# Attention and expert layer on one core: row maxima of pairs 2 to 8 handed on in two pieces, and three pieces of early work moved between engines

## The chip, the core and the metric

The kernel runs on one core of a Trainium2 chip. The core has five engines, each with its own instruction stream that runs in order: TensorE (PE, matrix products into PSUM), VectorE (DVE), ScalarE (ACT), GpSimd (POOL) and SyncE (SP, which here issues most of the DMAs). The metric is the device time of one execution in microseconds, lower is better.

## The reference, cut to what matters

```python
q_pool = q.reshape(B, H, S // 2, 2, D).mean(axis=3)       # B 8, H 8, S 1152, D 64
scores = scale * np.matmul(q_pool, k.transpose(0, 1, 3, 2))   # 576 queries x 1152 keys
scores = scores - np.max(scores, axis=-1, keepdims=True)
attn = np.exp(scores); attn = attn / (np.sum(attn, axis=-1, keepdims=True) + 1e-09)
x = np.matmul(attn, v)         # to (B * 576, 512), token major
# then a layer of 8 experts: each token goes to the expert with the largest
# logit (x @ w_gate + bias of its modality), 512 -> 1024 -> 512 with a ReLU,
# and is weighted with that expert's softmax probability
```

## The kernel before, in words

**Pairs and steps.** The 64 heads are worked in 32 pairs, numbered from 0; the two heads j=0 and j=1 of a pair lie in the upper and lower 64 partitions. `attention` writes a program in 18 steps per pair, 576 in all. Three steps make the scores of three key chunks of 128 for all 576 queries of one head: four PSUM banks of 432 columns, each a pair of products (L1051, L1052). So a pair has 36 products of L1051, the first 18 for j=0, and its first one marks the pair's start in the trace. ACT turns each bank into exponentials (L1053, `Pe`), and the lower halves of the exponentials' bits become a second f16 operand `Pl` (`lower`, L1034 on ACT or L1036 on DVE): of 1728 columns, 1152 go to ACT and 576 to DVE, but for pair 0 (`P_LIST = {0: 2}`) both pieces go to ACT. The value products (`pv`, L1110 to L1112, groups of three) follow some steps later.

**Maxima.** A product needs a bound of each query's scores first, which is the row maximum. `maxpass` makes it for one pair as 21 pieces: for each of nine groups u of 128 queries two products of 512 keys (L984), each reduced by one DVE instruction (L985), and for the last 128 keys three products with up to four groups side by side (L992, L993). These go through three PSUM buffers `pm`. `row` then reduces three numbers per query (L935), turns them with a small product (L949), scales them (L958, tile `mr`), and SP copies the result into row 64 of the operand `B2` (L959), which L1052 reads. For pair 1 (`TWO_ROWS = (1,)`) this is done twice: after five groups (1x5x128, enough for head j=0) and after nine (1x4x128, wanted by j=1); for other pairs once (1x9x128). Pair 0's first five groups are a prologue of their own (`first_max`, L1007, L1008), after `sum_q` has added the two query halves in two pieces.

**Order.** PE's order is written out by the string of a step in `ORD`: M is one piece of the maxima queue `mxq`, X a variable number of pieces, s a score bank, v a group of value products. M stands three times in three steps, X once in each. The pieces of a pair enter `mxq` from step 18p - 24 on. `at`, `later` and `later_end` place everything else at step numbers; SP's and POOL's instructions stand in the order in which they are written, and wait only for data.

```python
advance(mxq, 3 if t < T_F else 1 if t < X_ALL or t % (X_IN if t < X_SOME else 4) == 0 or len(mxq) > 1 else 0)
need(p, *(("place",) if p else ()), "row5" if j == 0 and (p == 0 or p in TWO_ROWS) else "row9")
```

The first line is the X of step t; the second, in `scores`, says which of the rows must have been written into the program. `place` and `place_rest` copy a pair's operands to where the products read them (L739, 12 DMAs a pair for pair 2), and `load_hi` loads f16 keys of pair 4 and later by a DMA from POOL's queue (L795). After the attention the experts run (`experts`), from about 720 us on.

Of the kernel before, what the change touches and what calls it, by code (L numbers as in the profile page):

```python
# [16 lines left out]
ALU = mybir.AluOpType  # L17
# [37 lines left out]

LOWS = (((0, 1152, 'A', 2), (1152, 1728, 'D', 3)), ((0, 1152, 'A', 2), (1152, 1728, 'D', 3)))
LOWS_LAST = (((0, 864, 'D', 1), (864, 1728, 'D', 3)),)
P_LIST = {0: 2}
LOWS_LIST = [tuple(((0, 1152, 'A', 2), (1152, 1728, e, 3)) for e in x) for x in ('DDA', 'DA', 'A')]
D0 = 5  # L60
T_RT = (20, 35, 43, 61)
D2 = (1, 0, 0, 0, 3)
T_K2 = 0
T_F = 7
T_P2 = 1
T_P1 = 8
T_M1 = 5
# [4 lines left out]
T_CAST = -36  # L72
# [73 lines left out]
DONE = object()  # L146
ORD = ('NvJMvsvMsvXF', 'JvvsMvvXFvv', 'vFvvsJvXv')
FIRST = (0, 1)
T_PRE = 2
TWO_ROWS = (1,)  # L150
X_ALL = 8
X_SOME = 105
X_IN = 3
T_MX2 = -23
T_MX3 = -23
FIN = 0
# [541 lines left out]
def attention(tc, ctx, att, ident, npairs, xpool, on_two, on_split, on_scale, jobs, side, set_pm, started, ahead, hip, own_port):  # L698
# [3 lines left out]
    nc = tc.nc  # L702
# [38 lines left out]
    half_q = lambda i: slice(i * 288, (i + 1) * 288)  # L741
# [409 lines left out]
    mxq, pvq, scq = [], [], []  # L1151
# [20 lines left out]
    def advance(q, n):  # L1172
        for _ in range(n):
            while q and next(q[0], DONE) is DONE:
                q.pop(0)
# [16 lines left out]
    def busy(n, w=512):  # L1192
        for _ in range(n):
            nc.tensor.matmul(idle[:, 0:w], zero[:, 0:P], zero[:, 0:w], start=True, stop=True, skip_group_check=True)
# [22 lines left out]
    first = first_max(0)  # L1217
    both = st[0]["q"].rearrange("p (w n) -> p w n", w=2)

    def sum_q(i):  # L1220
        nc.vector.tensor_tensor(both[:, 0, half_q(i)], both[:, 0, half_q(i)], both[:, 1, half_q(i)], op=ALU.add)
        nc.scalar.copy(qb[0:D, half_q(i)], q0[0:D, half_q(i)])

    sum_q(0)
    for i in range(3):
        split_hi(0, i)
        if i == 2:
            sum_q(1)
        for _ in range(2):
            next(first)  # L1230
        if i < 2:
            busy(1 + i)
    nc.scalar.copy(st[0]["qh"], q0)
    nc.scalar.copy(qb[D:P, SQ:S], q0[D:P])
    for i in (3, 4, 5, 6, 0, 1, 2):
        split_lo(0, i)
    st[0]["B1"] = pa.tile([P, 2 * KQ], F16, name="B1")
    place_k(0, (0,))
# [34 lines left out]
    mxq.append(maxpass(0, mp0))  # L1273
    for _ in range(T_PRE):
        advance(mxq, 1)
    busy(1)
    for t, f in zip(T_RT, started):
        at(t, 0, f)

    for p in range(npairs):  # L1280
        b = NSTEP * p
        go = lambda t, f, *a, p=p, b=b, **k: at(b + t, p, lambda: f(p, *a), **k)
        if p > 1:
            d = D2 if p == 2 else (0,) * 5
            if p < 4:
                go((T_K2, T_K3)[p - 2] - b, load_kq, end=False)
            go(T_SPLIT[p > 2] + d[0], split_q)
            go(T_QH[p > 2] + d[1], split_qh)
            if p > 3:
                go(T_CAST, load_hi)  # L1290
            else:
                for i in range(2):
                    go(T_HI[i] + d[2], split_hi, i)
            for i in range(3):
                go(T_LO[p > 2][i] + d[3], split_lo, i)
            go({2: T_MX2, 3: T_MX3}.get(p, T_MAX), lambda p: mxq.append(maxpass(p)), end=False)
            go(T_PLACE + (T_P2 if p == 2 else 0), place, end=False)
            if p > 2:
                go(T_REST, place_rest, end=False)
            go(T_LV[max(0, min(p, 4) - 2)], load_v)  # L1300
        elif p:
            go(T_P1 - b, place, end=False)
            go(T_M1 - b, lambda p: mxq.append(maxpass(p)), end=False)
            go(T_LV[max(0, min(p, 4) - 2)], load_v)
        sq, power_, vh, vs, vl = (T_SQ, T_POW, T_VH, T_VS, T_VL) if p > 1 else V1
        if p == 0:
            at(VS0, 0, lambda: shifted(0))
            continue
        if p == 1:
            go = lambda t, f, *a, p=p: at(t, p, lambda: f(p, *a))  # L1310
        go(sq, square)
        go(power_, power)
        for i, t in enumerate(vh):
            go(t, values, i, False)
        go(vs, shifted)
        for i, t in enumerate(vl):
            go(t, values, i, True)
# [14 lines left out]
    for t in range(NSTEP * npairs):  # L1332
        p, c18 = divmod(t, NSTEP)
        now[0] = t
        if jobs and c18 in JOBS:
            running.append(jobs.pop(0))
        for a in ORD[t % len(ORD)]:
            if a == "J":
                running[:] = [g for g in running if next(g, DONE) is not DONE]
            elif a == "F":  # L1340
                flush(t)
            elif a == "M":
                advance(mxq, 1)
            elif a == "X":
                advance(mxq, 3 if t < T_F else 1 if t < X_ALL or t % (X_IN if t < X_SOME else 4) == 0 or len(mxq) > 1 else 0)
            elif a == "N":
                scq.append(scores(p, *divmod(c18 // 3, 3)))
            elif a == "s":
                advance(scq, 1)
            elif a == "v":  # L1350
                advance(pvq, 2 if len(pvq) > 2 else 1)
        ends(t)
        if side and t >= wait:
            r = next(side[0], DONE)
            if r is DONE:
                side.pop(0)
            else:
                wait = t + (r or 1) if (r or 1) > 0 else NSTEP * npairs + r
# [484 lines left out]
```

## Time and profile before

| | us |
|---|---|
| median of three runs (1108.71 to 1110.17) | 1109.09 |
| the profiled execution's own time | 1109.55 |
| its span in the profile | 1107.8 |
| PE, DVE, ACT, POOL busy in the span | 1094.6, 951.4, 880.1, 449.2 |

The span is that of the instructions of one execution. PE's busy time counts matmuls whose ends are modelled and overlap, so a stretch in which PE is called busy can still hold small waits; how far apart two instructions start is the better measure. An idle time in square brackets in the rows below names what ended it.

### The profile page before, as it was taken

Reading aid. Unit: us, or ns where it says so; the run is one execution under the profiler, and the core shown is the slowest. Engines: PE = TensorE matmul, PEld = TensorE weight load, DVE = VectorE, ACT = ScalarE, POOL = GpSimd, SP = SyncE. Lnnn points to the kernel's source line nnn. Section 1 sums busy time; section 2 is a strip of 40 time slices with the busy share of each in tenths; the row PEclk is TensorE's granted clock in tenths of the full one; section 3 lists DMA queues with packets and bytes.
Section 4 is the critical chain, followed back from the end, with each engine's and each line's share of the span. In section 5 each row is a group of like instructions: output and inputs, shape, how many; then the busy total and the mean of one; then the engine's idle time right before and its main releaser. Section 6 shows DMA issues by size and latency. Waiting matters only on the chain. (4 is left out here: it accounts for less than half of the span.)

```text
span 1107.8 us, 36760 instructions
## 1 busy us (share of the span) xinstructions
PE 1094.6 (99%) x15134; PEld 812.5 (73%) x15134; DVE 951.4 (86%) x1897; ACT 880.1 (79%) x1397; POOL 449.2 (41%) x484
## 2 busy tenths in 40 slices
PE   8999999999999999999999999999999999999998
PEld 4777777777777777777777777876677667667666
DVE  8899999999999999999999999888987666756751
ACT  6999999999999999899999999876656565655652
POOL 8765444454545455545544454132122232121111
PEclk9999999999999999999999999999999999999999
DMA  8788867777678678687786775699989999999970
GB/s 252 184 189 213 200 174 192 198 196 195 171 212 203 174 197 205 162 205 179 214 190 174 213 160 120 185 298 313 275 257 232 304 312 289 272 279 270 280 209 33
DMA packets 178356, 237.59 MB, mean 214 GB/s; under 512 B 91555, under 2 KB 127027, under 8 KB 178180
## 3 DMA queue, kind: packets, MB, share of 16 engines
q1 hardware_dynamic: 168004, 207.12, 67.9%
q0 software_dynamic: 10176, 28.05, 11.4%
q8 instruction: 120, 1.97, 0.8%
q14 instruction: 56, 0.46, 0.2%
HBM read 158.43 MB, written 18.99 MB: 160 GB/s over the span
## 5 line engine op out<-in xcount | busy, mean ns | idle before, releaser
L1053 ACT ACTIVATE Pe<-psc 128x432 int32<-128x432 f32 x768 | 383.0, 526 | 51.0 <-PE psc L1052 32.2
L985 DVE TENSOR_REDUCE mp<-pm 128x1 f32<-128x512 f32 x566 | 372.9, 684 | 13.6 <-PE pm L984 6.8
L1111 PE MATMUL xp<-VS,Pl 128*128 128x65 f16 x2880 | 374.6, 194 | 0.0
L1110 PE MATMUL xp<-VH,Pe 128*128 128x65 f16 x2880 | 372.9, 193 | 0.0
L1112 PE MATMUL xp<-vl,Pe 128*128 128x64 f16 x2880 | 370.4, 191 | 0.0
L1111 PEld LDWEIGHTS <-Pl 128*128 128x128 f16 x2880 | 267.2, 97 | 86.3
L1051 PE MATMUL psc<-B 128*128 128x432 f16 (+2 forms) x1152 | 301.8, 285 | 0.9 <-ACT Pe L1053 0.8
L1052 PE MATMUL psc<-B 128*128 128x432 f16 (+5 forms) x1152 | 301.7, 286 | 0.0
L1110 PEld LDWEIGHTS <-Pe 128*128 128x128 f16 x2880 | 271.3, 98 | 41.0 <-issue 2.9
L1112 PEld LDWEIGHTS <-Pe 128*128 128x128 f16 x2880 | 268.8, 98 | 0.0
L1034 ACT ACTIVATE Pl<-Pe 128x1152 f16<-128x1152 uint16 x192 | 220.6, 1149 | 6.1
L984 PE MATMUL pm<-hi,QB 128*128 128x512 f16 x566 | 213.7, 378 | 1.9 <-DVE mp L985 1.2
L1497 PE MATMUL ph<-xpart,w1l 128*128 128x256 f16 x544 | 148.3, 273 | 0.0
L1496 PE MATMUL ph<-xpart,w1h 128*128 128x256 f16 x544 | 148.3, 273 | 0.0
L1495 PE MATMUL ph<-xpart,w1h 128*128 128x256 f16 x544 | 148.3, 273 | 0.0
L818 POOL TENSOR_TENSOR lo<-rawk,hi 128x576 f16<-128x576 f32 (+1 forms) x68 | 83.2, 1225 | 155.3 <-DVE Pl L1036 131.1
L1052 PEld LDWEIGHTS <-B 128*128 128x128 f16 (+1 forms) x1152 | 112.0, 97 | 23.0 <-issue 1.3
L1051 PEld LDWEIGHTS <-B 128*128 128x128 f16 x1152 | 111.5, 97 | 5.8 <-issue 0.7
L918 POOL TENSOR_SCALAR VH<-rawv,scales 128x512 f16<-128x512 f32 (+1 forms) x63 | 109.1, 1733 | 15.6 <-DVE Pl L1036 13.9
L1501 DVE SCALAR_TENSOR_TENSOR hl<-ph,hh 128x512 f16<-128x512 f32 x72 | 49.7, 690 | 70.3 <-ACT hh L1500 55.6
L1500 ACT ACTIVATE hh<-ph 128x512 f16<-128x512 f32 x72 | 43.0, 597 | 81.3 <-PE ph L1497 81.3
L1614 PE MATMUL po<-w2h,hl 128*128 128x512 f16 x280 | 106.1, 379 | 0.0
(326 smaller groups left out, 1885.5 us busy)
## 6 DMA issues: line engine op xcount, KB each, us to landing
w2r<-in_w_dram SPq DMA_DIRECT2D x72, 512.0 KB
w1r<-in_w_dram SPq DMA_DIRECT2D x68, 512.0 KB
rawv<-in_att_dram SPq DMA_DIRECT2D x32, 576.0 KB
B<-hi SPq DMA_DIRECT2D x128, 144.0 KB
rawq<-in_att_dram SPq DMA_DIRECT2D x31, 576.0 KB
rawk<-in_att_dram SPq DMA_DIRECT2D x31, 576.0 KB
B<-qh SPq DMA_DIRECT2D x128, 72.0 KB
B<-lo SPq DMA_DIRECT2D x64, 144.0 KB
```

Of the source, the lines that this page charges most:

```text
L984: nc.tensor.matmul(pm, QB[p % 2][:, u], s["hi"][:, t * 512:(t + 1) * 512], start=True, stop=True)
L985: nc.vector.tensor_reduce(mp[:, u, t:t + 1], pm, op=ALU.max, axis=AX.X)
L1034: nc.scalar.activation(low, rest, AF.Copy, scale=LOW)
L1051: nc.tensor.matmul(o, b1[:, ks], b1[:, qs], start=True, stop=False, skip_group_check=True)
L1052: nc.tensor.matmul(o, b2[:, ks], b2[:, qs], start=False, stop=True, skip_group_check=True)
L1053: nc.scalar.activation(Pe[:, D + x0:D + x1], pt, AF.Exp, scale=1.0 / 16)
L1110: nc.tensor.matmul(out, Ph[:, qs], vh[:, c, j, 0:D + 1], start=c == 0 and g == 0, stop=False, skip_group_check=True)
L1111: nc.tensor.matmul(out, Pl[:, qs], vs[:, c, j, 0:D + 1], start=False, stop=False, skip_group_check=True)
L1112: nc.tensor.matmul(out[:, 0:D], Ph[:, qs], vl[:, c, j], start=False, stop=c == NKC - 1, skip_group_check=True)
L1495: nc.tensor.matmul(o, hi[:, c, fs], xh[:, :, c], start=c == 0, stop=False)
L1496: nc.tensor.matmul(o, hi[:, c, fs], xl[:, :, c], start=False, stop=False)
L1497: nc.tensor.matmul(o, lo[:, c, fs], xh[:, :, c], start=False, stop=c == 3)
```

## The change

Six things change. (1) `TWO_ROWS` becomes pairs 1 to 7, so six more pairs (the second to the eighth, without the one that had it) hand on their maxima in two pieces, each with an L935, L949, L958 and L959 of its own. (2) The rate of X: three pieces a step only in steps 0 and 1 (was 0 to 6), one piece a step until step 7 as before, then one in steps divisible by 4 (was 3), and the extra piece when two pairs are in the queue only from step 105 on. One piece (was two) stands ahead of the first step. (3) Pair 0's lower halves of 576 columns go to DVE. (4) The second `sum_q` runs on POOL, behind two of POOL's four key splits in place of on DVE. (5) One filler product (`busy(1)`) ahead of the first step goes. (6) `load_hi` of pairs 4 to 9 stands five steps later.

```diff
-P_LIST = {0: 2}
+P_LIST = {}
-T_F = 7
+T_F = 2
-T_PRE = 2
-TWO_ROWS = (1,)
+T_PRE = 1
+TWO_ROWS = tuple(range(1, 8))
-X_IN = 3
+X_IN = 4
-    def sum_q(i):
-        nc.vector.tensor_tensor(both[:, 0, half_q(i)], both[:, 0, half_q(i)], both[:, 1, half_q(i)], op=ALU.add)
+    def sum_q(i, eng):
+        eng.tensor_tensor(both[:, 0, half_q(i)], both[:, 0, half_q(i)], both[:, 1, half_q(i)], op=ALU.add)
         nc.scalar.copy(qb[0:D, half_q(i)], q0[0:D, half_q(i)])
-    sum_q(0)
+    sum_q(0, nc.vector)
     for i in range(3):
         split_hi(0, i)
         if i == 2:
-            sum_q(1)
+            for k in (3, 4):
+                split_lo(0, k)
+            sum_q(1, nc.gpsimd)
...
-    for i in (3, 4, 5, 6, 0, 1, 2):
+    for i in (5, 6, 0, 1, 2):
         split_lo(0, i)
...
     for _ in range(T_PRE):
         advance(mxq, 1)
-    busy(1)
...
             if p > 3:
-                go(T_CAST, load_hi)
+                go(T_CAST + (5 if p - 2 in TWO_ROWS else 0), load_hi)
...
-                advance(mxq, 3 if t < T_F else 1 if t < X_ALL or t % (X_IN if t < X_SOME else 4) == 0 or len(mxq) > 1 else 0)
+                advance(mxq, 3 if t < T_F else 1 if t < X_ALL or t % (X_IN if t < X_SOME else 4) == 0 or len(mxq) > 1 and t >= X_SOME else 0)
```

On POOL, in the prologue (`rawq` are the queries, `rawk` the keys, `lo` their second f16 part), the difference is:

```order
 L1197 MEMSET B_1_113 1x1152
-L818 TENSOR_TENSOR lo<-rawk,hi 128x288 x4
+L818 TENSOR_TENSOR lo<-rawk,hi 128x288 x2
+L1221 TENSOR_TENSOR rawq<-rawq 128x288
+L818 TENSOR_TENSOR lo<-rawk,hi 128x288 x2
 L818 TENSOR_TENSOR lo<-rawq,qh 128x192 x3
 L771 TENSOR_TENSOR rawq<-rawq 128x576
```

The sum of the second query halves stands third in this group, and DVE's stream lost it.

On DVE, in pair 0 from the end of its second group of maxima on, there stood before:

```order
L993 TENSOR_REDUCE mp<-pm 128x4
L935 TENSOR_REDUCE m_393<-mp 128x4
L929 TENSOR_SCALAR VS_124<-VH_123 128x18x64
L958 TENSOR_SCALAR mr<-pj 4x128
L985 TENSOR_REDUCE mp<-pm 128x1 x8
L993 TENSOR_REDUCE mp<-pm 128x4
```

and there stands now:

```order
L935 TENSOR_REDUCE m_392<-mp 128x4
L1036 TENSOR_SCALAR Pl_116<-Pe_115 128x576
L929 TENSOR_SCALAR VS_124<-VH_123 128x18x64
L958 TENSOR_SCALAR mr<-pj 4x128
L985 TENSOR_REDUCE mp<-pm 128x1 x4
L1036 TENSOR_SCALAR Pl_118<-Pe_117 128x576
L985 TENSOR_REDUCE mp<-pm 128x1 x4
L993 TENSOR_REDUCE mp<-pm 128x4
L1036 TENSOR_SCALAR Pl_120<-Pe_119 128x576
```

Lower halves (L1036) now stand between the reductions; pair 0 has six of them.

On SP, around the rows of pair 1 (`mr` into B_1_113) and the copies for pair 2 (into B_0_111 and one more `B`), there stood before:

```order
L739 DMA QB_112<-qh 64x576 x2
L959 DMA B_1_113<-mr 1x5x128
L761 DMA rawv<-in_att_dram 128x1152
L959 DMA B_1_113<-mr 1x4x128
L756 DMA rawq<-in_att_dram 128x1152
L757 DMA rawk<-in_att_dram 128x1152
L739 DMA B_0_111<-qh 64x576 x2
L739 DMA B_924<-qh 64x576 x2
L739 DMA B_924<-lo 64x576 x2
L739 DMA B_0_111<-lo 64x1152 x2
L739 DMA B_924<-hi 64x1152 x4
L190 DMA wg<-in_w_gate_dram 128x4x8
```

and there stands now:

```order
L761 DMA rawv<-in_att_dram 128x1152
L959 DMA B_1_113<-mr 1x5x128
L739 DMA B_0_111<-qh 64x576 x2
L739 DMA B_893<-qh 64x576 x2
L739 DMA B_893<-lo 64x576 x2
L739 DMA B_0_111<-lo 64x1152 x2
L739 DMA B_893<-hi 64x1152 x4
L190 DMA wg<-in_w_gate_dram 128x4x8
L192 DMA bias<-in_bias_dram 128x16
L194 DMA idt<-in_ids_dram 128x72
L761 DMA rawv<-in_att_dram 128x1152
L959 DMA B_1_113<-mr 1x4x128
```

Pair 1's second row was ahead of pair 2's twelve copies and now stands behind them, three small loads and a load of values.

## Rows read from the trace of the kernel before

**Rows 1.** The page's busy us, share of the span and instructions by engine.
```profile
PE 1094.6 (99%) x15134; PEld 812.5 (73%) x15134; DVE 951.4 (86%) x1897; ACT 880.1 (79%) x1397; POOL 449.2 (41%) x484
```

**Rows 2.** Busy time by stretch: pair 0, pair 1, pairs 2 to 6, pairs 8 and 9.
```profile
16.69:41.87 25.18, 22.97 (x302) 15.64 (x301) 22.01 (x46) 22.49 (x39) 19.20 (x17) 1.00 0.77 222
41.87:66.48 24.61, 23.42 (x398) 17.82 (x397) 23.21 (x47) 22.21 (x37) 16.39 (x12) 1.00 0.73 175
66.48:175.64 109.16, 108.85 (x1896) 84.51 (x1895) 104.86 (x219) 100.69 (x170) 57.89 (x73) 1.00 0.81 196
197.53:240.84 43.31, 43.31 (x764) 33.76 (x763) 41.52 (x88) 40.06 (x68) 21.88 (x23) 1.00 0.75 189
```

**Rows 3.** Groups of PE instructions by line, from 16.69 to 66.48 us.
```profile
L1110 PE MATMUL xp<-VH,Pe 128*128 128x65 f16 x159 | 21.3, 193 | 0.0
L984 PE MATMUL pm<-hi,QB 128*128 128x512 f16 x47 | 17.4, 378 | 1.2 <-DVE mp L985 1.2
L992 PE MATMUL pm<-hi,QB 128*128 128x128 f16 x22 | 2.4, 218 | 0.6 <-DVE mp L985 0.6
```

**Rows 4.** Timeline of PE: start us, us, then the instruction.
```profile
9.79 0.34 PE L1007 MATMUL pm<-hi,QB 128*128 128x384 f16 x1 [1.14 <-DVE mp L1008]
...
23.05 0.34 PE L1051 MATMUL psc<-B 128*128 128x432 f16 x1 [0.48 <-ACT Pe L1053]
...
23.42 0.81 PE L984 MATMUL pm<-hi,QB 128*128 128x512 f16 x3
...
32.11 0.27 PE L949 MATMUL pm<-ident,m 128*5 128x128 f32 x1
32.22 0.19 PE L1110 MATMUL xp<-VH,Pe 128*128 128x65 f16 x1
...
32.30 0.19 PE L1110 MATMUL xp<-VH,Pe 128*128 128x65 f16 x1
...
41.87 0.35 PE L1051 MATMUL psc<-B 128*128 128x432 f16 x1
...
54.38 0.34 PE L1051 MATMUL psc<-B 128*128 128x432 f16 x1
```

**Rows 5.** Timeline of POOL.
```profile
6.86 2.10 POOL L818 TENSOR_TENSOR lo<-rawk,hi 128x288 f16<-128x288 f32 x3 [0.85 <-ACT hi L802]
...
48.56 1.11 POOL L912 TENSOR_TENSOR vl<-rawv,VH 128x512 f16<-128x512 f32 x1
```

**Rows 6.** Timeline of DVE.
```profile
8.28 0.99 DVE L1221 TENSOR_TENSOR rawq<-rawq 128x288 f32<-128x288 f32 x1
...
16.41 4.85 DVE L985 TENSOR_REDUCE mp<-pm 128x1 f32<-128x512 f32 x8
...
41.68 0.28 DVE L958 TENSOR_SCALAR mr<-pm 4x128 f16<-4x128 f32 x1
...
48.59 1.41 DVE L1036 TENSOR_SCALAR Pl<-Pe 128x576 f16<-128x576 uint16 x1
```

**Rows 7.** Timeline of ACT.
```profile
21.90 0.68 ACT L1034 ACTIVATE Pl<-Pe 128x576 f16<-128x576 uint16 x1
```

**Rows 8.** Instructions of L1036 up to 110 us: ns min/median/max, first and last start.
```profile
L1036 DVE TENSOR_SCALAR Pl<-Pe x17: 446/450/1407, 48.6 to 108.9; 128x576 f16<-128x576 uint16 x17
```

**Rows 9.** Timeline of SP's queue: each start is when the DMA is issued.
```profile
37.53 0.77 SPq L959 DMA_DIRECT2D B<-mr  x1
...
41.99 0.66 SPq L959 DMA_DIRECT2D B<-mr  x1
...
43.70 2.50 SPq L739 DMA_DIRECT2D B<-qh  x4
46.30 3.28 SPq L739 DMA_DIRECT2D B<-lo  x4
49.69 3.81 SPq L739 DMA_DIRECT2D B<-hi  x4
...
55.31 0.37 SPq L761 DMA_DIRECT2D rawv<-in_att_dram  x1
```

## The prediction, made before the changed kernel was run

> **What bounds the kernel now.** I read the page's busy times first: PE is busy in 99% of the span, DVE in 86% [rows 1]. So the end can come earlier in two ways only: less work on PE, or fewer waits of PE. The change takes one filler of 512 columns from PE and adds six small turns, so any gain has to come from waits, and the next view is the busy time by stretch, cut where pairs start [rows 2]. Pairs 8 and 9 take 43.31 us with PE busy in all of it: 21.66 us a pair is PE's own pace. Pairs 2 to 6 take 21.83 us each, close to it. Pairs 0 and 1 take 25.18 and 24.61 us. They don't hold the same work, so I counted it: 159 groups of value products, 46 maxima products of 512 keys and 22 of 128 (a product that straddles the border makes 47 of the 46) [rows 3], where two steady pairs have 180, 36 and 18. The price of each is the distance between starts: 0.08 us for a group, (0.81 - 0.38) / 2 = 0.215 for a product of 512 keys, a quarter of that for one of 128, 0.11 for a turn [rows 3, 4]. At PE's own pace the two pairs would take 43.31 - 21 x 0.08 + 10 x 0.215 + 4 x 0.054 + 2 x 0.11 = 44.2 us. They take 49.79, so **5.6 us are lost in waits before 66.48 us**, and 1.1 us more in the prologue, in the one wait there that this change touches (the product at 9.79) [rows 4]. After that almost nothing is left to win: 109.16 - 5 x 21.66 = 0.9 us in pairs 2 to 6, and from pair 7 on the two programs have the same work in the same order.
>
> **The prologue.** The product at 9.79 waits for the second half of the queries. DVE adds it from 8.28 to 9.27, behind four reductions. POOL has its second split done at 6.86 + 0.70 = 7.56, and a sum of the same 288 columns, taken at the split's 0.70, ends at 8.26 [rows 5, 6]. That is 1.0 us earlier, and DVE, whose reductions follow without a gap, gets 0.9 to 1.0 back. I take -0.9 for the start of pair 0; the bounds are 0 (if the sum meets DVE's reads) and the whole wait, -1.1. The filler lies just ahead of the first scores: -0.2 there at most; the first exponential waits for other work of the same chain, so I count none of it.
>
> **Pair 0.** Six lower halves go from ACT, where one lasts 0.68 us [rows 7], to DVE, where one lasts 0.45 when nothing is beside it. The waits for ACT, as the one at 23.05 [rows 4], should go. DVE gives up three reductions (25 products of 512 keys are issued ahead of pair 1 now, from 2 at pair 0's start; before it was 29, from 3), a group of short ones and a row, 3 x 0.60 + 0.68 + 0.45 [rows 6] (a row is 0.28 at L958 and, as an estimate from that, 0.17 at the smaller L935), and takes 6 x 0.45: 22.01 - 2.9 + 2.7 = 21.8 us. PE has 62 groups there and less of the maxima, 20 us. So neither engine keeps pair 0 at 25 us. One thing may: at 48.59 a lower half took 1.41 us, while POOL worked on one instruction from 48.56 to 49.67, and POOL is busy for 19.20 us of pair 0 [rows 2, 5, 6]. Of 17 lower halves up to 110 us the median is 0.45 and the longest 1.41 [rows 8], so I add 6 x 0.4 (between none and 0.96 each, nearer to the median): DVE 24.2 us if it waits for nothing else, of which 1.5 can lie behind PE's back, in the three buffers `pm`.
>
> The Trainium skill (SBUF — State Buffer, Who interferes with whom) says that such a DVE instruction and one of GpSimd exclude each other for the whole instruction, whoever comes first. The long row agrees; by the rule alone, with POOL busy three quarters of the time, all six would wait and pair 0 would gain nothing, which is the third rival below.
>
> **The rows of pair 1 in SP's queue.** SP is in order, so a row's issue time is set by what stands ahead of it. The first row (1x5x128) went out at 37.53, 4.3 us ahead of its use at 41.87, behind pair 1's own copies [rows 4, 9]. Those follow pair 0's chain, so they can come at most the prologue's 0.9 earlier; a load of values is now ahead of the row too (0.4, as the one at 55.31). With half of the 0.9 the row goes out at 37.5 again. It lands between 0.77 (its own time) and 4.5 us (its use) later; no row shows it, and I take 1.5, since it is 1 KB. So **pair 1 can't start before 39.0**, and PE and DVE would be there at about 38. I take 38.9: 3.0 us gained so far. The second row stood at 41.99. It now follows twelve copies, three small loads and the load of values, which took from 43.70 to 55.68, 12.0 us; at the pace of the first four copies (0.62 each) it would be 9.6. From 38.2 on that gives an issue at 47.8 to 50.2, and with 1.5 a landing at 49.3 to 51.7. PE wants it for head j=1, half a pair later: 54.38 - 41.87 = 12.5 us before, and at PE's own pace (21.66 + 7 x 0.08 + 0.215 + 0.11 = 22.6) 11.3, so at 50.2. I take a wait of 0.5 us (0 to 1.5). Pair 2 then starts at 38.9 + 22.6 + 0.5 = **62.0**, which is **-4.5**.
>
> **What is given back.** The slower rate moves work, it takes none away: 44 and 18 maxima products stand ahead of pair 2 now, 49 and 22 before, so 5 x 0.215 + 4 x 0.054 = +1.3 us come back by pair 7, where both programs stand at 140 and 67. Six more turns cost PE 6 x 0.11 = +0.7. And DVE, busy for 104.86 us of pairs 2 to 6, gets 5 x 0.60 + 0.68 + 6 x 0.45 = 6.4 more, 111.2 us, in a stretch that PE fills with 109.16 + 2.0 = 111.1. DVE counts an instruction's overlapping tail as busy (0.68 long, 0.60 apart), so it isn't full at that, but it isn't free either: steady pairs have it at 96%, by which the stretch would take 115.8, +4.7. I take +0.9 (0 to 4.7), near the lower end, since the reductions now come evenly and not in bursts. `load_hi` has its data wanted by PE over 10 steps later and is hidden by that; the later loads of keys (behind pair 1's second row) by 15 steps. Without that cover each would cost what its lateness is, microseconds.
>
> **The sum** is -4.5 + 1.3 + 0.7 + 0.9 = **-1.6 us**, against the profiled execution's 1109.55 (1107.8 in the span and 1.75 around it). That execution stands 0.46 above the median, so the forecast for the median is 1109.09 - 1.6 = **1107.5 us**. A change of 0.2%, 2.2 us, is about what a measurement of this kernel can tell from none.
>
> **The rivals.** *The rows and the port stay out of the way*: pair 1 starts at PE's pace, near 37.3, pair 2 at 59.9, and DVE costs 0.3 in pairs 2 to 6: -6.6 + 2.0 + 0.3 = -4.3, 1104.8 us. For it speaks that the copies' pace depends on loads ahead of them which now stand behind; against it the 4.3 us that the first row has in hand, less than the gain it would need. *The second row is stuck*: if it goes out at 50.2 and lands 4.5 later, at 54.7, head j=1 of pair 1 waits 4.5 us in place of 0.5, and the sum is +2.4: 1111.5, slower. It decides from an issue later than about 48.7. *POOL holds the port*: each lower half waits 0.96, DVE has 27.6 us in pair 0, the start of pair 1 stays near 41.9, pair 1 still gains its 1.5: -1.5 + 2.9 = +1.4, and with DVE at its worse price after that +2.5 or more: 1111.6. *The lower rate does nothing*, because DVE bounds pairs 0 to 6 as a whole: then only the prologue is left, -0.9 + 0.7, no change.
>
> **How the numbers follow.** My forecast and the case that nothing changes, which end on the same side of 0.2%, get 0.34 and 0.10; the clear gain 0.40; the stuck row 0.10; the port 0.06. So faster 0.40, same 0.44, slower 0.16. The likeliest case's own range, from its bounds, is 1106 to 1109; the clear gain lies around 1104.8 and the slower cases around 1111.5, and with half of the one and a third of the other outside, the range is 1104.3 to 1110.6.
>
> **What would show it.** In the changed profile: the seventh L1007 near 8.8 instead of 9.79; pair 1 near 38.9, pair 2 near 62.0, pair 7 near 174.0 (175.64 before); the idle time ahead of L1051 no longer named after ACT in pair 0; six L1036 before 41 us with a mean near 0.85; the 1x4x128 row of pair 1 issued at 48 to 50, and the L1052 of head j=1 held up by a DMA or not; DVE's busy share of pairs 2 to 6 near 99%. The prediction is wrong if pair 2 starts outside 60.5 to 64, or if pairs 2 to 6 take more than 113.5 us.

## The result: 1% slower, and the profile after

The changed kernel takes **1120.1 us** (median of 4; 1119.07 to 1122.27) against 1108.9 for the kernel before on the same chip: a ratio of 1.0098, 95% interval 1.0086 to 1.0110. The forecast was 1107.5, in a range that ended at 1110.6. It missed the range and the sign.

The profiled execution took 1122.27 us, 1120.6 of them in the span. Its busy times by engine, which answer to [rows 1]:

```profile
PE 1097.3 (98%) x15139; PEld 813.8 (73%) x15139; DVE 953.0 (85%) x1914; ACT 879.2 (78%) x1391; POOL 447.1 (40%) x485
```

The engines have nearly the work they had. What grew is PE's idle time. The stretches of [rows 2], cut anew where pairs start (pair 0, pair 1, pairs 2 to 6, pairs 8 and 9; columns: length, busy us of PE, PEld, DVE, ACT and POOL with instructions, granted clock, DMA share, GB/s):

```profile
15.71:37.95 22.24, 21.20 (x293) 14.97 (x294) 20.36 (x44) 20.48 (x35) 20.08 (x17) 1.00 0.82 227
37.95:69.31 31.36, 26.30 (x398) 19.71 (x397) 22.25 (x48) 21.90 (x36) 15.38 (x12) 0.89 0.57 140
69.31:187.96 118.65, 111.81 (x1911) 85.88 (x1910) 109.98 (x238) 102.14 (x169) 57.89 (x73) 1.00 0.75 185
209.84:253.16 43.32, 43.32 (x764) 33.76 (x763) 41.53 (x88) 40.05 (x68) 21.87 (x23) 1.00 0.76 191
```

Pair 0 starts 1.0 us earlier and is 2.9 us shorter: at 37.95 the changed kernel is 3.9 us ahead. Pair 1 then takes 31.4 us in place of 24.6 and pairs 2 to 6 take 118.7 in place of 109.2. From pair 7 on the pace is the old one. So the loss lies in 150 us, and most of it is waits of PE: in pairs 2 to 6 PE is idle for 118.65 - 111.81 = 6.8 us, before for 0.3. VectorE's share there fell, from 96% to 93%, so by its share it did not become the bound. By the prediction's own signs it failed on both: pair 2 starts at 69.31 (60.5 to 64 was allowed), and pairs 2 to 6 take more than 113.5 us.

**The row of pair 1 lands late.** PE's timeline: pair 1's first score product, then the one that reads the row of maxima.

```profile
37.95 0.35 PE L1051 MATMUL psc<-B 128*128 128x432 f16 x1
41.24 0.34 PE L1052 MATMUL psc<-B 65*128 65x432 f16 x1 [2.94 <-DMA B<-mr]
```

SP's queue (each start is an issue) has that row directly behind a load of values, and the second row at 48.67:

```profile
36.67 0.58 SPq L761 DMA_DIRECT2D rawv<-in_att_dram  x1
37.34 0.78 SPq L959 DMA_DIRECT2D B<-mr  x1
...
48.67 0.67 SPq L959 DMA_DIRECT2D B<-mr  x1
```

The row went out at 37.34 and released its reader at 41.24, **3.9 us** later, for 1.2 KB.

**Idle stretches are followed by the lower clock.** Busy times and granted clock of the wait above, of a second idle stretch, and of what came behind each:

```profile
37.95:41.24 3.29, 0.35 (x5) 0.10 (x4) 0.90 (x2) 0.33 (x1) 3.29 (x3) 1.00 0.76 236
41.24:44.99 3.75, 3.75 (x41) 3.05 (x41) 1.96 (x4) 3.02 (x6) 1.58 (x2) 0.55 0.69 160
...
56.10:58.60 2.50, 0.88 (x16) 0.54 (x13) 2.46 (x7) 2.44 (x4) 0.77 (x1) 1.00 0.95 127
58.65:62.06 3.41, 3.26 (x29) 2.08 (x30) 1.07 (x3) 0.53 (x1) 0.46 (x1) 0.50 0.28 58
```

PE was busy for 0.35 of 3.29 us and for 0.88 of 2.50; each time the granted clock was 0.50 (1.2 in place of 2.4 GHz) for 3.41 us soon after. As an estimate, half of the 3.41 us is lost each time, about 1.7 us. Pair 1's second product starts 3.29 us after its first, where the kernel before has 0.19 (41.87 and 42.06). So the late row costs 3.1 us and some 1.7 more.

**PE waits at the turns.** Waits from 37.95 to 187.96 us (total us, times, longest):

```profile
PEld pm L949 <- DVE m L935: 10.0, 10, 1.7
PE pm L949 <- DVE m L935: 8.4, 10, 1.6
```

L949 is the small product that turns a row of maxima. PE runs in order, so while it waits, everything behind it waits too. VectorE's timeline ahead of the longest of these waits:

```profile
56.10 0.68 DVE L993 TENSOR_REDUCE mp<-pm 128x4 f32<-128x512 f32 x1
56.70 0.68 DVE L985 TENSOR_REDUCE mp<-pm 128x1 f32<-128x512 f32 x1
57.30 0.45 DVE L1036 TENSOR_SCALAR Pl<-Pe 128x576 f16<-128x576 uint16 x1
57.66 0.69 DVE L985 TENSOR_REDUCE mp<-pm 128x1 f32<-128x512 f32 x1
58.26 0.28 DVE L993 TENSOR_REDUCE mp<-pm 128x1 f32<-128x128 f32 x1
58.58 0.17 DVE L935 TENSOR_REDUCE m<-mp 128x5 f32<-128x15 f32 x1
```

And the turn on PE:

```profile
58.80 0.38 PE L949 MATMUL pm<-ident,m 128*5 128x128 f32 x1 [1.57 <-DVE m L935]
```

The last product of the row had been made at 56.84, but VectorE had three instructions ahead of its reduction (L985, L1036, L985). Between that product and the turn PE had six instructions. A row in two pieces has two such places per pair, and the turn stands 6 to 16 PE instructions behind the last product at most of them; in the kernel before most rows had 15 to 47. Of these waits 6.8 us lie in pairs 2 to 6 on PE, and 8.3 on its weight loads.

**VectorE's lower halves in pair 0** (ns min/median/max):

```profile
L1036 DVE TENSOR_SCALAR Pl<-Pe x5: 449/450/796, 21.0 to 35.7; 128x576 f16<-128x576 uint16 x5
```

These are five of the six; the sixth ran at 42.71, in pair 1. One of the five was held up, by 0.35 us. Another ran in the middle of a GpSimd instruction, which the wait of L929 shows to have ended at 21.9, and still took 0.45:

```profile
20.11 1.79 POOL L918 TENSOR_SCALAR VH<-rawv,scales 128x512 f16<-128x512 f32 x1
...
20.98 0.45 DVE L1036 TENSOR_SCALAR Pl<-Pe 128x576 f16<-128x576 uint16 x1
21.93 0.46 DVE L929 TENSOR_SCALAR VS<-VH 128x1152 f16<-128x1152 f16 x1 [0.50 <-POOL VH L918]
```

So the rival in which GpSimd holds the port did not happen here, and the two engines did not exclude each other for every such instruction.

### The profile page after: what moved, and what is told of

Same layout as the page of the kernel before. It is cut to its first block, busy times and chain, and to the rows that moved or that the text cites. A ratio compares the mean times of both kernels' runs of the same rounds, so it can differ in the third digit from the quotient of the medians.

```text
span 1120.6 us, 36829 instructions
## 1 busy us (share of the span) xinstructions
PE 1097.3 (98%) x15139; PEld 813.8 (73%) x15139; DVE 953.0 (85%) x1914; ACT 879.2 (78%) x1391; POOL 447.1 (40%) x485
## 5 line engine op out<-in xcount | busy, mean ns | idle before, releaser
L985 DVE TENSOR_REDUCE mp<-pm 128x1 f32<-128x512 f32 x566 | 373.7, 684 | 23.6 <-PE pm L984 17.0
L1034 ACT ACTIVATE Pl<-Pe 128x1152 f16<-128x1152 uint16 x186 | 216.5, 1164 | 5.9
L1052 PEld LDWEIGHTS <-B 128*128 128x128 f16 (+1 forms) x1152 | 112.3, 97 | 21.9 <-issue 0.3
```

Of the source, the lines that this page charges most:

```text
L985: nc.vector.tensor_reduce(mp[:, u, t:t + 1], pm, op=ALU.max, axis=AX.X)
L1034: nc.scalar.activation(low, rest, AF.Copy, scale=LOW)
L1052: nc.tensor.matmul(o, b2[:, ks], b2[:, qs], start=False, stop=True, skip_group_check=True)
```

## The experiments

Two theories stood at first: A, two separate new waits (the late row, the turns); B, VectorE is the bound of pairs 0 to 6 as a whole.

**early_parts.** Rows and rate as before; only the sum on GpSimd, the lower halves on VectorE, one filler less and one early piece of maxima less are new. (The later `load_hi` hangs on `TWO_ROWS`, so it goes back with it.)

```diff
-T_F = 2
-TWO_ROWS = tuple(range(1, 8))
-X_IN = 4
+T_F = 7
+TWO_ROWS = (1,)
+X_IN = 3
...
-                advance(mxq, 3 if t < T_F else 1 if t < X_ALL or t % (X_IN if t < X_SOME else 4) == 0 or len(mxq) > 1 and t >= X_SOME else 0)
+                advance(mxq, 3 if t < T_F else 1 if t < X_ALL or t % (X_IN if t < X_SOME else 4) == 0 or len(mxq) > 1 else 0)
```

> Of the change only the early parts: the second sum on POOL, pair 0's lower halves on DVE, one filler and one early piece less. The rate of the maxima and the single two-piece pair are as before the change. Theory A: these parts are not what costs; they give 0 to 3 us against the kernel before, 1106 to 1109. Theory B: six more instructions on DVE in pair 0 meet a full DVE, and the time is 1110 or more.

Measured: 1108.12 us, 0.9990 (0.9978 to 1.0001). Pair 0 starts at 15.45, pair 7 at 174.56 (before 16.69 and 175.64). So in the profiles these parts gain 1.1 us; the medians' interval just includes no change. The whole loss is in the rows and the rate.

**row_first.** The load of values behind the row of pair 1.

```diff
-T_LV = (-24, -34, -36)
+T_LV = (-20, -34, -36)
```

> The changed kernel with one number changed: the load of pair 2's values is written four steps later, so that in SP's queue pair 1's first row (1x5x128) stands ahead of it, as before the change. Theory A (two separate new waits, one for this row behind a large load, one at each turn of a row): the row lands about 1.5 us after its issue in place of 3.9, L1052 at the start of pair 1 waits under 1 us in place of 3.1, the low clock after it goes, and the time falls by 3 to 5 us from 1120.1, to 1115 to 1117. Theory B (DVE bounds pairs 0 to 6 as a whole, and waits only show where PE meets it): PE waits for DVE elsewhere, and the time stays at 1119 to 1121.

Measured: 1119.35 us, 1.0088 (1.0067 to 1.0109). In its profile the wait at the start of pair 1 and both stretches at the lower clock are gone and pair 1 takes 26.24 us (31.36), but the second row is waited for (1.1 us), and pairs 2 to 6 take as long as in the changed kernel:

```profile
64.22:183.97 119.75, 112.12 (x1912) 86.00 (x1911) 111.09 (x238) 102.24 (x169) 58.02 (x73) 1.00 0.74 184
```

Pair 7 starts 4.0 us earlier than in the changed kernel's profile, but the median is only 0.8 lower. The profiled execution is the shortest of this kernel's and was the longest of the changed one's, so the medians decide. A's number is missed, B's (1119 to 1121) is met.

**turn_later** and **both.** Turns of all pairs two steps later (`FIN`), alone and with row_first.

```diff
-FIN = 0
+FIN = 2
```

> The changed kernel with one number changed: from step 19 on the turn of a row (L949) and what follows is written two steps later than its reduction, for all pairs. Theory A: the ten waits of L949 for DVE's L935 in pairs 1 to 6 (0.4 to 1.7 us each, about 10 us together) mostly go, with the low clock after the longest of them, and the time falls by 6 to 9 us, to 1111 to 1114. Theory B: the same waits come back ahead of L984, which waits for one of three buffers; pairs 2 to 6 still take 117 us or more, and the time stays over 1117.

> Both numbers changed together. Theory A: the two gains add, 10 to 13 us from 1120.1, so 1107 to 1110, about the time of the kernel before or a little under it. Theory B: over 1116.

Measured: 1119.88 us (1.0087, 1.0056 to 1.0118) and 1122.10 us (1.0117, 1.0093 to 1.0141). The waits at the turns are gone, and others took their place; both times are where B put them. `FIN` also delays the transposes of x, and PE waits for those, 2.0 us in turn_later and 3.6 in both, again with the lower clock behind. From turn_later:

```profile
102.65 0.59 PE L287 MATMUL pm<-wgs,xt 128*128 128x24 bf16 x17 [1.97 <-DMA xt<-x]
```

The edit moved two things, so it could not tell why.

**turn_two.** Only the turns of pairs 2 to 7 move.

```diff
+        if 1 < p and p in TWO_ROWS:
+            later_end(0, lambda: [turns.pop(0)() for _ in range(len(turns))])
...
-                    later_end(FIN if now[0] > NSTEP else 1, row(p, mp, 0, 5))
+                    later_end(2 if p > 1 else FIN if now[0] > NSTEP else 1, row(p, mp, 0, 5))
...
-        later_end(FIN if now[0] > NSTEP else 3 if p == 0 else 2, row(p, mp, u0, 9))
+        later_end(2 if two and p > 1 else FIN if now[0] > NSTEP else 3 if p == 0 else 2, row(p, mp, u0, 9))
```

> The changed kernel, but the transposes that turn a row of maxima are written two steps later for both rows of pairs 2 to 7; the transposes of x, pair 1, and pairs 8 on stay where they are, so that the transfer wait of turn_later has no reason to come. Theory A (two separate waits): the waits of the turn on DVE, about 9 us in sum, go; some 2 us come back as work that stood behind them; pairs 2 to 6 take 109.5 to 113 us; 1112 to 1115 us. Theory B (VectorE is full in pairs 0 to 6 as a whole): the waits move to other products; pairs 2 to 6 take over 115 us; over 1117 us.

Measured: 1118.26 us, 1.0070 (1.0053 to 1.0087). A is missed again and B's numbers are met, but the profile names a new wait, on VectorE's timeline:

```profile
180.34 0.28 DVE L961 TENSOR_SCALAR mr<-pm 4x128 f16<-4x128 f32 x1 [4.08 <-DMA B<-mr]
```

SP's queue at that place:

```profile
174.40 0.75 SPq L962 DMA_DIRECT2D B<-mr  x1
175.25 3.24 SPq L1098 DMA_TRANSPOSE xt<-x  x2
180.65 0.65 SPq L962 DMA_DIRECT2D B<-mr  x1
```

`mr` has one buffer. The copy of the first row was issued at 174.40 and freed it at 180.34, 5.9 us later; until then VectorE could not write the second row, and all its reductions stood behind that write.

**rows_first** and **turn_rows.** Pair 1's first row ahead of the load of pair 2's values, its second row behind that load and ahead of the copies for pair 2; the second run has turn_two as well.

```diff
-T_RT = (20, 35, 43, 61)
-T_P2 = 1
-T_LV = (-24, -34, -36)
+T_RT = (22, 35, 43, 61)
+T_P2 = 2
+T_LV = (-20, -32, -36)
```

> The changed kernel, but both rows of maxima of pair 1 stand in SP's queue ahead of the large load of v and of the copies of q, k and lo; the turns are left as they are. Theory A: the wait of 3.3 us at the start of pair 1 and the one of 2.8 us before pair 2 go, with the stretches at the lower clock behind them (about 3.4 us together); pair 2 starts at 61 to 64 us; the turns keep their 9 us; 1113 to 1117 us. Theory B: the start of pair 2 moves forward and pairs 2 to 6 take as much longer; pair 7 at 184 us or later; over 1118 us.

> Both of the above in one kernel. Theory A: the gains add, since they lie in different stretches: 1106 to 1110 us, pair 7 at 173 to 177 us. Theory B: no better than turn_two alone; over 1114 us.

Measured: 1121.80 us (1.0109, 1.0092 to 1.0126) and 1122.31 us (1.0120, 1.0102 to 1.0138). Now the load is late: ACT's square of v waits 3.7 us for it and PE's L876 waits for the square, 2.9 us at 43.17 in rows_first, with the lower clock behind it. In each of the three orders of the queue that were run (the changed kernel's, row_first's and this one) something is late. A's sums do not add, and B's numbers are met.

**old_rate.** Two rows for pairs 1 to 7, the rate of before: early_parts without its edit of `TWO_ROWS`.

```diff
-T_F = 2
+T_F = 7
...
-X_IN = 4
+X_IN = 3
```

> The changed kernel with two rows kept for pairs 1 to 7, but the rate of the first steps and the distance of x as before the change (T_F 7, X_IN 3, and the old condition on the first groups). Theory A (the turn is written too close behind the last reduction, and the row stands behind a load; the lower rate has no price of its own): the same waits as in the changed kernel, 1117 to 1121 us. A rival C: it is the lower rate that brings VectorE late to the last reduction of a row; then the waits of the turn in pairs 2 to 6 fall under 4 us in sum and the time is 1110 to 1115 us. Theory B: 1117 us or more, with VectorE's share over 97% in pairs 2 to 6.

Measured: 1113.80 us, 1.0040 (1.0026 to 1.0054). With early_parts this divides the loss: from 1108.1 **the two rows (with the later `load_hi`) add 5.7 us, and the lower rate 6.3 more**. The three kernels ran on different chips; by their ratios to the kernel before it is 5.5 and 6.4. Pairs 2 to 6 by engine:

```profile
64.44:178.39 113.95, 110.05 (x1902) 85.02 (x1900) 106.59 (x229) 101.06 (x170) 57.73 (x73) 1.00 0.79 188
```

And the waits at the turns in them, which nearly halved:

```profile
PEld pm L949 <- DVE m L935: 4.7, 6, 0.9
...
PE pm L949 <- DVE m L935: 3.9, 6, 0.8
```

On PE they are just under the 4 us of rival C, on the weight loads they are over it; C's time is met. VectorE's share is 94%, where theory B wanted over 97%, and B's time is missed.

**tf_only** and **xin_only.** The two halves of the rate: tf_only keeps `T_F = 2` and has the other edits of old_rate, its condition too; xin_only has this edit alone:

```diff
-T_F = 2
+T_F = 7
```

> The changed kernel with one half of its lower rate: T_F stays 2 (fewer groups of maxima in steps 2 to 6), the rate after that (X_IN and the condition on a second pass) is that of before. Old_rate, without both halves, took 1113.8 us. Theory D (each half has its own price: T_F ends pair 0 three us earlier but brings the row of pair 1 behind the load; the rate after step 8 makes the turns wait): pair 0 takes 22 to 23 us, the wait of some 3 us at the start of pair 1 and its stretch at the lower clock are there, pairs 2 to 6 take 113 to 115 us as in old_rate; 1113 to 1117 us. Theory B (the sum of the work of VectorE decides, not the place): as in the changed kernel, over 1118 us.

> The other half: T_F 7 as before the change, X_IN 4 and the new condition as in the changed kernel. Theory D: no wait of 3 us at the start of pair 1; pairs 2 to 6 take 116 to 120 us, since the turns wait as in the changed kernel; 1115 to 1119 us. Rival E (all of the price of the rate comes from T_F): pairs 2 to 6 take 113 to 115 us; 1112 to 1115 us.

Measured: 1121.70 us (1.0121, 1.0104 to 1.0138) and 1117.09 us (1.0068, 1.0052 to 1.0085). Pairs 2 to 6 take 113.9 and 112.6 us in their profiles, both near old_rate's 113.95; only the two halves together gave 118.7. Each half alone loses its time in pair 1 (29.6 and 30.8 us; old_rate 24.1), at a turn behind VectorE. PE's timeline in tf_only:

```profile
54.13 0.27 PE L949 MATMUL pm<-ident,m 128*5 128x128 f32 x1 [2.75 <-DVE m L935]
```

And in xin_only:

```profile
56.71 0.38 PE L949 MATMUL pm<-ident,m 128*5 128x128 f32 x1 [3.24 <-DVE m L935]
```

Xin_only's time is in theory D's range, its pairs 2 to 6 are under D's and E's. Tf_only's pairs 2 to 6 are where D put them, but its median is over D's range and where B put it. Its four times go from 1116.85 to 1123.96, and the profile is of the shortest; what the longer ones lose isn't in a trace. Xin_only's profile is of its longest, which lost 3 us ahead of pair 0 as told under early_v30.

**old_rate_turn** and **old_rate_turn_mr.** Old_rate with turn_two's edit, then with a second buffer too.

```diff
-            mr = sm.tile([9, P], F16, name="mr", bufs=1)
+            mr = sm.tile([9, P], F16, name="mr", bufs=2)
```

> Old_rate (two rows for pairs 1 to 7, rate of before) with the turns of pairs 2 to 7 two steps later, as in turn_two. Old_rate has six waits of the turn of 0.7 to 0.9 us, about 4.9 us in sum, and took 1113.8 us. Theory D: these waits go and nothing takes their place, since VectorE is ahead; 1108.5 to 1111.5 us. Theory B: the row comes too late or other products wait; 1112.5 us or more.

> Old_rate_turn (two rows, rate of before, turns of pairs 2 to 7 two steps later; 1114.7 us) with two buffers for the row mr. Theory F (VectorE waited for the one buffer): pair 2 takes 21.8 to 22.5 us in place of 27.1, pair 6 under 22.4 in place of 23.2; pairs 2 to 6 within 1 us of before (109.2 us); 1107.5 to 1110 us. Rival G (the rows' copies themselves are late, and the products wait for them): the wait moves from VectorE to TensorE, and the time stays over 1112 us.

Measured: 1114.71 us (1.0047, 1.0029 to 1.0066), with waits for `mr` of 3.0 us in pair 2 and 1.8 in pair 6; then **1109.27 us** (0.9995, 0.9987 to 1.0004). Pairs 2 to 6 with the second buffer:

```profile
64.67:173.96 109.29, 109.21 (x1901) 84.86 (x1900) 104.90 (x229) 100.51 (x170) 58.10 (x73) 1.00 0.87 200
```

PE is idle for 0.1 us in 109.29, with two rows in each pair. Theory F holds: with both edits two rows cost nothing that can be measured. That undoes B for the rows: VectorE does all the work of old_rate here. The single buffer is no cost of the changed kernel or of old_rate, though: in neither does VectorE wait for `mr`. It costs once the turns stand later, so the repair takes both edits; the second buffer without the late turns was not run.

**turn_mr.** The same two repairs at the lower rate.

> Turn_two (the changed kernel with its lower rate, turns two steps later; 1118.3 us) with two buffers for mr. Theory F: the waits of 2.9 us at 86 us and 3.5 us at 177 us and their stretches at the lower clock go, the start of pair 1 keeps its own wait; 1109 to 1113 us. Theory B (with the lower rate VectorE is full in pairs 2 to 6): pairs 2 to 6 take 113 us or more, over 1114 us.

Measured: 1117.28 us, 1.0069 (1.0053 to 1.0086). Theory F is missed and B's two numbers are met: the rate alone costs 8.0 us against old_rate_turn_mr, and pairs 2 to 6 take 115.85 us. But VectorE works 109.79 us in them, 95%, a smaller share than before the change, and 2.9 us ahead of pair 1's second product and 2.3 in pair 3 are waits for a row's copy. So I still had a theory H to try: those two waits are the price.

**repaired_2** and **repaired_1.** Turn_mr with row_first's edit (the first hunk); repaired_1 has the other two as well, turns one step later.

```diff
-T_LV = (-24, -34, -36)
+T_LV = (-20, -34, -36)
...
-                    later_end(2 if p > 1 else FIN if now[0] > NSTEP else 1, row(p, mp, 0, 5))
+                    later_end(1 if p > 1 else FIN if now[0] > NSTEP else 1, row(p, mp, 0, 5))
...
-        later_end(2 if two and p > 1 else FIN if now[0] > NSTEP else 3 if p == 0 else 2, row(p, mp, u0, 9))
+        later_end(1 if two and p > 1 else FIN if now[0] > NSTEP else 3 if p == 0 else 2, row(p, mp, u0, 9))
```

> Turn_mr with the load of v behind the row of pair 1, as in row_first. Theory H (the price of the lower rate is two waits for a row's copy, each with a stretch at the lower clock): the one at the start of pair 1 goes, 4 to 5 us; the one at the start of pair 3 stays; 1111 to 1114 us. Theory B (VectorE): pair 2 starts earlier and pairs 2 to 6 take as much longer; over 1115 us.

> The same with the turns one step later in place of two. Theory H: the row of pair 3 is issued by 84.5 us and the wait at its start falls under 1 us, at the price of turns that wait some 0.3 us each; pairs 2 to 6 take 110 to 112.5 us; 1107 to 1111 us. Theory B: pairs 2 to 6 take 113 us or more; 1113 us or more.

Measured: 1116.21 us (1.0052, 1.0039 to 1.0065) and 1115.62 us (1.0055, 1.0038 to 1.0072). Neither reaches theory H's number, and both lie where B put them. The rows say what is late, though. Repaired_2 loses most in pair 3 (26.57 us), over its second row, which VectorE scales at:

```profile
92.00 0.27 DVE L961 TENSOR_SCALAR mr<-pm 4x128 f16<-4x128 f32 x1
```

SP's queue holds it up:

```profile
88.83 0.35 SPq L761 DMA_DIRECT2D rawv<-in_att_dram  x1
89.28 3.79 SPq L1098 DMA_TRANSPOSE xt<-x  x2
93.16 2.47 SPq L739 DMA_DIRECT2D B<-qh  x4
95.72 2.10 SPq L739 DMA_DIRECT2D B<-lo  x2
97.92 0.68 SPq L962 DMA_DIRECT2D B<-mr  x1
```

And PE waits for it:

```profile
101.82 0.34 PE L1056 MATMUL psc<-B 128*128 128x432 f16 x1 [2.30 <-DMA B<-mr]
```

The row was written by 92.27, issued at 97.92 and released PE at 101.82. The transposes and copies ahead of it hold SP for 5.6 us, then it needs 3.9 to land. At the rate of before the row is written four to five maxima products earlier, and nothing waits. In repaired_1 the row of pair 3 was issued at 87.71, 5 us after it was written, and PE waited 1.9 us for it: one step earlier does not help in a queue that is late itself. It also lost 3.2 us in pair 1 to the load of values, as rows_first did.

Pair by pair, repaired_2 answers theory B better than its median. Pairs 2, 3, 5 and 6 of repaired_2:

```profile
65.18:87.64 22.46, 22.14 (x381) 17.13 (x380) 22.01 (x48) 20.10 (x34) 14.67 (x26) 1.00 0.82 205
87.64:114.21 26.57, 24.25 (x395) 18.30 (x394) 22.33 (x50) 20.61 (x34) 13.00 (x20) 0.94 0.69 159
...
136.58:158.78 22.20, 22.20 (x396) 17.30 (x395) 21.52 (x49) 20.01 (x34) 9.98 (x9) 1.00 0.61 163
158.78:180.53 21.75, 21.75 (x378) 16.84 (x377) 21.07 (x48) 20.27 (x36) 10.00 (x9) 1.00 0.88 214
```

Pair 3 takes 4.4 us more than in old_rate_turn_mr (22.21), the other four pairs of 2 to 6 together 1.7. In pairs 2, 5 and 6 VectorE works for 97% to 98% of the time, more than before the change, and PE is idle for 0.3 us at most; in pair 3 VectorE works for 84%, and there the row is late.

**early_v30.** Early_parts with one load of values behind two copies that PE waited for.

```diff
-T_LV = (-24, -34, -36)
+T_LV = (-24, -30, -36)
```

> Early_parts (rows and rate as before the change; only the sums on GpSimd, the lower halves and the order of the start are new), with the load of v for pair 3 issued behind the copies of the queries of pair 2, not ahead of them. Early_parts has one new wait there: 1.36 us at 61.4 us, a product waits for that copy. If that wait is the load's doing, pair 2 starts at 64.0 to 64.6 and the time is 1105.5 to 1107.5 us, under both kernels; if the queue is late for another reason, 1107.5 to 1109 us.

Measured: 1108.24 us, 0.9987 (0.9977 to 0.9998), the lowest ratio of the study; its interval ends just under 1, but 0.13% is about as little as a measurement here can tell from nothing. The wait of 1.2 us went (pair 1 takes 23.56 us, 24.82 in early_parts), so it was the load's doing, but the time is not in the range that was to follow from that. The profiled execution, the longest of ten, starts pair 0 at 18.58, 3 us late. VectorE's timeline in the prologue:

```profile
13.53 3.38 DVE L938 TENSOR_SCALAR first_m<-m 128x5 f16<-128x5 f32 x1
```

GpSimd's at the same time:

```profile
14.10 2.78 POOL L818 TENSOR_TENSOR lo<-rawk,hi 128x288 f16<-128x288 f32 x4
```

The same instruction takes 0.56 us in early_parts, where it ended at 14.20 and GpSimd's four began at 14.22. Here it ended with the fourth. The granted clock fell to 0.50 from 17.02 to 20.43. Of the 18 profiles that have the instruction on VectorE one more, xin_only's, shows this.

**early_best** and **two_best.** That instruction on GpSimd, ahead of some memsets and the four, which stood before `drain`; two_best has it in old_rate_turn_mr, with early_v30's edit.

```diff
-            nc.vector.tensor_scalar(first_m[:, :, D], m9[:, 0:n], 1.0 / ROW, 16.0 * math.log(PSC) / ROW, op0=ALU.mult, op1=ALU.add)
+            nc.gpsimd.tensor_scalar(first_m[:, :, D], m9[:, 0:n], 1.0 / ROW, 16.0 * math.log(PSC) / ROW, op0=ALU.mult, op1=ALU.add)
...
     drain(first)
+    if npairs > 1:
+        for pe, pl in PT:
+            for x in (slice(0, D), slice(D + W3, 2 * D + W3)):
+                nc.gpsimd.memset(pe[:, x].bitcast(F32), 0.0)
+                nc.gpsimd.memset(pl[:, x], 0.0)
+        for i in (3, 4, 5, 6):
+            split_lo(1, i)
```

> Early_v30 with the small scaling of the first row on GpSimd, ahead of the memsets and the four lower halves that follow it there. If VectorE's instruction was held up by GpSimd's run in some executions: the spread falls from 3.5 us to under 2, pair 0 starts at 14.6 to 15.6 us, 1105 to 1107 us, under both kernels. If the spread comes from elsewhere: 1107 to 1110 us with the old spread.

> Old_rate_turn_mr with the two edits of early_best: two rows for pairs 1 to 7 with late turns and two buffers, the rate of before. Two rows bring nothing of their own at this rate, since no product waited for the single row in before: 1106 to 1109 us, level with early_best or up to 2 us over it. If the earlier first row is worth something, it is under early_best.

Measured: 1110.78 us (1.0002, 0.9992 to 1.0012) and 1110.84 us (1.0006, 0.9998 to 1.0015). Missed: early_best's twelve times span 4.8 us (early_v30's 3.5), so it is not shown that the held-up instruction makes the spread. Pair 0 does start earlier in early_best, at 14.77, but GpSimd's values of pair 0 are now later and PE waits for them:

```profile
23.39 0.19 PE L1111 MATMUL xp<-VS,Pl 128*128 128x65 f16 x1 [1.45 <-DVE VS L929]
```

So early_parts, early_v30, old_rate_turn_mr and these two are level with the kernel before and about 1% under the changed one, and none beats the kernel before by more than a measurement can tell.

## Why the prediction was wrong, step by step

**What bounds the kernel** was right: the engines' work is the same, and the change was decided by PE's waits ahead of pair 7.

**The prologue** was right: the seventh L1007 at 8.58 (forecast 8.8), pair 0 1.0 us earlier (0.9). **Pair 0** was right in its effect: it takes 22.2 us, with the lower halves at 0.45 in the median. The term of 6 x 0.4 for GpSimd was too high: 0.35 in all five. Pair 1 starts at 37.95. The forecast of 38.9 was the landing of the row; the first product of a pair doesn't read it, so the pair starts and its second product waits.

**"It lands between 0.77 and 4.5 us later; no row shows it, and I take 1.5, since it is 1 KB"** is the first step that failed. The issue time was right to 0.2 us (37.34 for 37.5; the second row 48.67 for 47.8 to 50.2). The landing took 3.9, near my upper bound; where a waiter shows the landing of such a row in other runs it was 2.0 (xin_only, 114.61 to 116.61) to 6.4 us (old_rate_turn, 171.57 to 177.97). The Trainium skill (SBUF — State Buffer, The DMA setup-cost knee) gives every transfer a fixed cost of about 2 us whatever its size. The rows that can be read here took from that to three times that. The wait at the start of pair 1 was 3.1 us, and the lower clock behind it 1.7, a cost that stood in no term. So pair 1 gave back more than pair 0 had won.

**"Six more turns cost PE 6 x 0.11 = +0.7"** is the second and larger one. I priced the turn at PE's own time and did not ask how close it stands behind the reduction that it waits for. In old_rate six turns wait 3.9 us on PE in pairs 2 to 6 and that stretch is 4.8 us longer than before; with the turns later and a second `mr` it is 0.1 longer. So the 0.7 was too high for the turns themselves and 4 us too low for where they stand. The one buffer of `mr`, which I also missed, is not in these 4 us; it stood in the way of the repair.

**"So 5 x 0.215 + 4 x 0.054 = +1.3 us come back"** prices the moved work only. Moving it also takes away the lead of the maxima: 44 products ahead of pair 2 in place of 49. With the lead went slack of the rows in SP's queue and of the turns behind VectorE: with the two repairs PE waits in pairs 1 to 6 for no row and 0.3 us for a turn at the old rate (old_rate_turn_mr), and for three rows (2.9, 2.3 and 0.3 us) and a turn (0.7) at the lower one (turn_mr). The lower rate costs 6.3 us in the changed kernel and 8.0 with the two repairs.

**DVE in pairs 2 to 6, +0.9 (0 to 4.7)**: the work came (109.98 us for 111.2), the share did not go to 99% but fell to 93%, so by the rows it is not VectorE's lack of time that costs. Its queue costs, where PE waits for one instruction in it. Theory B gave the right numbers for most low-rate kernels to the end, but for a reason that their rows don't show.

**The rivals.** The clear gain (0.40) failed on the landing. The stuck second row (0.10) had the right mechanism in a wrong place: rows stand behind SP's copies and land late, at the start of pair 1 and of later pairs. The port (0.06) was refuted for pair 0's lower halves; that all six would wait was also too much, with GpSimd busy for three quarters of the time. That the lower rate does nothing (0.10) failed too: it costs. The first three were worked out for pairs 0 and 1, and the fourth had no cost; beyond VectorE's share none had a mechanism that repeats in pairs 2 to 6, and that is where 9.5 of the 16 us lost since 37.95 lie.

**What stays open.** The low-rate kernels spread over 3 to 7 us, and only one execution of each is in a trace. Of the rate's price in repaired_2, 6.1 us in pairs 2 to 6 against old_rate_turn_mr, the late row (2.3) and, as an estimate, its low clock (1.7; 0.50 from 102.20 to 105.61) make 4.0; the rest is near the moved work of 1.3 but wasn't measured by itself. No run at the low rate came back to the time of before, so for the rate the cause is read from rows and not shown by a repair. Whether the large load ahead of pair 1's row or the busy queue as a whole makes its landing long was not told apart. A low rate with the rows in another engine's queue was not tried.

## What to carry to other kernels

An instruction in an in-order queue that waits for another engine costs what that other engine has in its queue, so read how many instructions stand between producer and consumer, and not only the consumer's duration. When work is put off to fill an earlier stretch, ask what its lead was covering: here five products of lead hid the landing of rows in a busy DMA queue, and part of what VectorE had ahead of each turn. A small copy behind large ones is priced by when it releases its reader in the nearest trace, and a gap in PE is priced with the low clock that follows it.

## What the runs showed of the hardware that was not expected

A copy of 1.0 to 1.2 KB released its waiter 3.9 us (37.34 to 41.24, and 97.92 to 101.82) to 5.9 us (174.40 to 180.34) after its issue, when loads, copies or transposes had been issued around it. Over all runs it was 2.0 to 6.4 us.

A VectorE instruction on 128x5 numbers took 3.38 us in place of 0.56 when it was under way at the start of a run of four GpSimd instructions, and it ended only with the fourth. The Trainium skill (SBUF — State Buffer, Who interferes with whom) says that the one that comes second is blocked for the other's whole instruction. Here four back to back passed it by, in two of 18 profiles; and a lower half in pair 0 was not blocked at all in the middle of a GpSimd instruction.

The idle stretches of 3.29 and 2.50 us in the changed kernel, with PE busy for 0.35 and 0.88 us of them, were followed by a granted clock of 0.50 for 3.41 us, and xin_only's wait of 3.24 us in pair 1 came with one of 0.50 from 55.90 to 62.72; tf_only's wait of 2.75 us in pair 1 was not followed by it, its clock stayed at 1.00.
